# Attention steps moved in front of the state-weight products of a fused attention and two-FFN kernel

## The chip, the cores and the metric

One core of a Trainium2 chip runs the whole program. The metric is the device time of one execution in microseconds (us), lower is better, as the median of a few runs. Alongside, one execution was recorded by the hardware profiler; its rows give start and length of every instruction on each engine: PE (TensorE matmuls), DVE (VectorE), ACT (ScalarE), POOL (GpSimd), SP (SyncE, which issues DMAs here).

## What is computed

```python
def _attn_ref(x, state):             # x (8, 8, 512, 64), state (8, 8, 32, 64)
    scores = scale * x @ state^T;     a = softmax(scores);   xread = a @ state
    scores2 = scale * state @ x^T;    a2 = softmax(scores2); sread = a2 @ x
    return concatenate([xread, sread], axis=2)
x = attention output, transposed and reshaped to (4352, 512)
x = relu(x @ w_in)**2 @ w_out        # first FFN, 2048 wide
out = ((x @ w1) * (x @ w2)) @ w3 @ w_out2
```

## The kernel before, in words

The 4352 tokens are 8 batches of 512 rows (xread) and one block of 256 rows (sread of all batches), all held transposed. xread is never formed: since xread @ w_in = a @ (state @ w_in), `make_sw` multiplies the state of a batch by 512 columns of w_in (the **state weights**, SW), and `h_tile(c, f)` then multiplies the attention weights `aT` by them: six matmuls of 128x128 by 512 columns give tile f (of 16) of batch c before the relu. `act_h` makes relu (L534), square (L536) and the high part of a split (L537) of it on ACT, and the low part (L538, tile `ghl`, kept in the list `done`) on DVE. `y_tile` multiplies that by w_out, twelve matmuls.

**The loop.** The list `order` holds 96 pairs (c, f), and the loop (L834) makes one h tile per index i, then the y tile of an earlier index (two of them behind a state-weight group), so one index takes six plus twelve matmuls. The attention of a batch b is cut into steps (`att_steps`), which hang on the indices of this loop: `scores` (sixteen small matmuls on tiles of 64 rows by 32 columns of the array, into both banks of the PSUM tag "m", then two copies to the tiles S), `soft2`, `soft1a`, `soft1b` (softmax pieces on DVE and ACT), `a_T` (a turn on DVE and a split), `a2_T` (four PE transposes and a copy, once for each half r), `sread` (64 matmuls of 64 columns on tiles of 128 rows by 32 columns, a DVE copy to the tile sr) and `sread_T` (one PE transpose and a copy into x9T). `att_slots` gives for each batch a list of steps per index, counted from the index where the batch starts (32, 48, 60, 72, 85 for batches 3 to 7, 5 for batch 2); they are put into `late`, which runs at the end of an index. The steps stand alone: scores, each `a2_T`, sread and sread_T each come at an index of their own.

**State-weight groups.** At the indices 15, 23, 31, ... 87 (`pairs`) `sw_pair` makes two `make_sw` directly behind the h tile, and at index 95 two more are made for batches 6 and 7. Each of these groups is 32 small matmuls on tiles of 64 rows by 32 columns, and each `make_sw` fills two PSUM banks: the first takes both banks of tag "m", the second both banks of tag "h", in which `h_tile` also makes its product. So the second `make_sw` reuses the bank of the h tile just finished, which relu has to have read.

**What sets the order.** A planner puts each engine's instructions into one fixed order when the kernel is built: of what is ready in its own model of the time it takes what comes first in the program. `tc.issue_after(m)` adds that what follows on the engine of m stands behind m. On the chip every engine then takes its instructions in that order and waits at each for its semaphores. An x block for the scores is loaded by `load_xb` (eight DMAs on SP), turned on DVE by `turn_x`; the x block for sread is loaded by `load_xn` into the tag "X" (two buffers), one DMA on SP.

Of the kernel before, what the change touches and what calls it, by code (L numbers as in the profile page):

```python
# [20 lines left out]
def kernel(  # L21
# [17 lines left out]
    nc = tc.nc  # L39
    B, H, S, D = x.shape  # L40
# [5 lines left out]
    P = 128  # L46
# [3 lines left out]
    NF = DF // P  # L50
# [14 lines left out]
    BLK, ALONE = 2, 3  # L65
    PAIR = (B - 2, B - 1)
# [14 lines left out]
    def bank_m(name):  # L81
        return psum.tile([P, 512], F32, tag="m", bufs=2, name=name)

    def bank_h(name):
        return psum.tile([P, 512], F32, tag="h", bufs=2, name=name)
# [221 lines left out]
    def load_xn(b, g):  # L307
        t = att.tile([P, HG, J, D], F32, tag="X", bufs=2, name=f"X{b}_{g}")
        nc.sync.dma_start(t, x[b, g * HG:(g + 1) * HG].rearrange("h (j p) d -> p h j d", p=P))
        X[b, g] = t.rearrange("p h j d -> p j h d")  # L310
# [9 lines left out]
    def att_steps(b):  # L320
# [3 lines left out]
        v = {}  # L324
# [15 lines left out]
        def scores():  # L340
            pss = [bank_m("ps_s") for _ in range(G)]
            for k in range(HG):
                for r in range(G):
                    rows = slice(r * D, (r + 1) * D)
                    mm = nc.tensor.matmul(
                        pss[r][k * NS:(k + 1) * NS, :], stT[rows, b, k, :], xT[b, k][rows, :],
                        start=True, stop=True, tile_position=(r * D, k * NS),
                    )
            scored.append(mm)
            for r in range(G):  # L350
                pool, tag, bufs = (att, "S", 2) if b else (wpool, "wo", NF)
                s = pool.tile([P, 512], F32, tag=tag, bufs=bufs, name="S")
                last = nc.scalar.copy(s, pss[r])
                v["S", r] = s
            return last

        def soft2(r):
            nm = att.tile([P, 1], F32, tag="nm", bufs=2, name="nm")
# [65 lines left out]
                nc.tensor.transpose(ps[:, j * P:(j + 1) * P], e[:, j * P:(j + 1) * P], ident)  # L424
            nc.scalar.copy(e, ps)

        def sread():
            ps = bank_m("ps_r")
            for r in range(G):
                for j in range(J):  # L430
                    for k in range(HG):
                        nc.tensor.matmul(
                            ps[k * NS:(k + 1) * NS, r * D:(r + 1) * D],
                            v["a2", r][:, j * P + k * NS:j * P + (k + 1) * NS],
                            X[b, k // 2][:, j, 2 * (k % 2) + r, :],
                            start=(j == 0), stop=(j == J - 1), tile_position=(0, k * NS),
                        )
            t = att.tile([P, G * D], F32, tag="sr", bufs=1, name="sr")
            nc.vector.tensor_copy(t, ps[:, 0:G * D])
            v["sr"] = t  # L440

        def sread_T():
            ps = bank_m("ps_rT")
            nc.tensor.transpose(ps[:, 0:P], v["sr"], ident)
            (nc.vector.tensor_copy if b < ALONE else nc.scalar.copy)(
                x9T[:, :, b * NS:(b + 1) * NS], ps[:, 0:P].rearrange("p (k n) -> p k n", n=NS),
            )

        def step(f, *args):
            return lambda: f(*args)  # L450
# [3 lines left out]
            *([step(f, r) for r in range(G)] for f in (soft2, soft1a, soft1b, a_T, a2_T)),  # L454
            sread, sread_T,
        )

    def att_slots(b, parts=None):
        if b >= B:
            return [[] for _ in range(NF)]  # L460
        xp, sc, s2, s1a, s1b, at, a2t, sr, srt = att_steps(b)
        if parts is not None:
            parts.extend((xp, sc, s2, s1a, s1b, a2t, at))
        if b > ALONE + 1:
            return [
                [sc], [], [s2[0], s1a[0]], [s1b[0], s2[1]], [a2t[0]], [at[0], s1a[1]],
                [a2t[1]], [s1b[1]], [sr], [at[1]], [srt],
            ]
        if b > ALONE:
            return [  # L470
                [sc], [], [s2[0], s1a[0]], [],
                [s1b[0], s2[1]], [a2t[0]], [at[0], s1a[1]], [a2t[1]],
                [s1b[1]], [sr], [at[1]], [srt], [], [], [], [],
            ]
        if b == ALONE:
            return [
                [sc], [], [s2[0], s1a[0]], [], [s1b[0], s2[1]], [a2t[0]], [], [a2t[1]],
                [at[0], s1a[1]], [sr], [s1b[1]], [srt], [at[1]], [], [], [],
            ]
        return [  # L480
            [], [], [], [], [], [s1a[0]], [s1b[0]], [at[0], s1a[1]],
            [s1b[1]], [at[1]], [s2[0]], [a2t[0], s2[1]], [], [a2t[1]], [sr], [srt], [],
        ]

    SW = {}
    last_sw = []
# [228 lines left out]
    def sw(b, fg):  # L715
        return lambda: make_sw(b, fg)

    def sw_pair(b, fg):
        make_sw(b, fg)
        make_sw(b, fg + 1, banks=lambda r, name: bank_h(name))  # L720

    side = {i: [] for i in range(NF * B)}
    late = {}
# [28 lines left out]
    for g in range(G):  # L752
# [1 line left out]
        side[4 + g].append(lambda g=g: load_xb(2, g))  # L754
        side[8 + g].append(lambda g=g: turn_x(2, g))
        side[11 + g].append(lambda g=g: load_xn(2, g))
    att2 = []
    for i, steps in enumerate(att_slots(2, att2)):
        late[5 + i] = steps

    def scores_and_sw():
        with tc.issue_after(h_mms[-1].ins):
            att2[1]()
        with tc.issue_after(scored[-1].ins):
            sw_low.append(make_sw(1, 1, banks=lambda r, name: bank_h(name)))

    side[10].append(scores_and_sw)
    behind_y, sw_low = {10: [srt1]}, []
    for b, i0 in zip(range(ALONE, B), (32, 48, 60, 72, 85)):
        for i, steps in enumerate(att_slots(b)):  # L770
            late.setdefault(i0 + i, []).extend(steps)
        for g in range(G):
            side[i0 - 8 + g].append(lambda b=b, g=g: load_xb(b, g))
            side[i0 - (6 if b < B - 1 else 3) + g].append(lambda b=b, g=g: turn_x(b, g))
            side[i0 - 2 + g].append(lambda b=b, g=g: load_xn(b, g))
    for g in range(G):
        side[80 + 3 * g].append(lambda g=g: load_aT(PAIR[0], g))

# [54 lines left out]
    order += [(c, f) for c in range(3, PAIR[0]) for f in range(NF)]  # L833
    for i, (c, f) in enumerate(order):  # L834
        h_tile(c, f)
        if i in pairs:
            sw_pair(*pairs[i])
        if i + 1 == len(order):
            make_sw(c0, 0)
            make_sw(c1, 0, banks=lambda r, name: bank_h(name))  # L840

        gate = done[i - 3] if i >= 8 else first
        with tc.issue_after(gate.ins):
            for job in side.get(i, ()):
                job()
        pend.append((c, f))
        while len(pend) > (1 if i in pairs else 2):
            last_y = y_tile(*pend.pop(0))
            with tc.issue_after(last_y.ins):
                for job in behind_y.pop(i, ()):  # L850
                    job()
        with ExitStack() as order_of:
            if i >= 8:
                order_of.enter_context(tc.issue_after(done[i - 3].ins))
            if i == 10:
                order_of.enter_context(tc.issue_after(sw_low[0].ins))
            if 10 <= i < 16:
                order_of.enter_context(tc.issue_after(casts[-1].ins))
            if i == max(pairs):
                order_of.enter_context(tc.issue_after(relus[-1].ins))  # L860
            for job in late.get(i, ()):
                job()
# [901 lines left out]
```

## Time and profile before

| | |
|---|---|
| median of 3 runs | 1193.29 us (1192.48 to 1193.63) |
| the profiled execution | 1194.18 us, of which the span from first to last instruction is 1192.4 us |
| PE busy | 1181.7 us (99%), 6400 matmuls |
| DVE, ACT, POOL busy | 967.6 us (81%), 695.9 us (58%), 191.8 us (16%) |
| granted TensorE clock | 0.999 of full speed |
| chain that ended last | PE 94%, DMA 2%, DVE 2%, ACT 1% |

The times are to be read with one care: matmuls are pipelined, so a line of the timeline lasts longer than the step to the next line. What a stretch of PE costs is the difference between the start of its first line and the start of the line behind it.

### The profile page before, as it was taken

What the parts mean: (1) busy time and instruction counts of PE and PEld (TensorE: products, weight loads), DVE (VectorE), ACT (ScalarE), POOL (GpSimd) and SP (SyncE); (2) the same over time, 40 slices, a digit from 0 to 9 for tenths busy, and PEclk for the clock granted to TensorE, in tenths of its full rate; (3) what the DMA queues carried; (4) which work ended last, traced back from release to release, by engine and by line L of the source; (5) the groups of instructions that cost most, each with busy time, mean ns of one, the idle gap of its engine ahead of it and who ended that gap; (6) DMA issues with size and microseconds to landing.
All of it is one profiled execution on the core that took longest, in us unless ns stands there. A gap on an engine that the chain in (4) does not pass through costs nothing.

```text
span 1192.4 us, 17909 instructions
## 1 busy us (share of the span) xinstructions
PE 1181.7 (99%) x6400; PEld 950.4 (80%) x6400; DVE 967.6 (81%) x1729; ACT 695.9 (58%) x1263; POOL 191.8 (16%) x277
## 2 busy tenths in 40 slices
PE   8999999999999999999999999999999999999998
PEld 5677777777787777777788888888888888888888
DVE  7989877778888774676778986989898968988987
ACT  6777556565656565876867753636364635363642
POOL 0000013323331200012231000120101030313030
PEclk9999999999999999999999999999999999999999
DMA  8575768936885932447697676653514382666576
GB/s 253 140 231 190 184 212 238 198 120 175 173 203 169 245 130 102 114 109 114 98 184 243 235 195 159 106 146 67 142 56 121 131 230 67 165 98 158 90 124 178
DMA packets 204722, 187.58 MB, mean 157 GB/s; under 512 B 120648, under 2 KB 156232, under 8 KB 204104
## 3 DMA queue, kind: packets, MB, share of 16 engines
q1 hardware_dynamic: 155848, 111.70, 33.1%
q0 software_dynamic: 46768, 71.32, 28.7%
q10 hardware_dynamic: 2016, 3.41, 0.8%
q8 instruction: 50, 0.82, 0.3%
q14 instruction: 40, 0.33, 0.1%
HBM read 122.81 MB, written 82.44 MB: 172 GB/s over the span
## 4 chain that ended last, share of the span: by engine, by line
PE 94%; DMA 2%; DVE 2%; ACT 1%; issue 0%; POOL 0%; SPq 0%; DVEq 0%; POOLq 0%; ACTq 0%
PE y L594 22%; PE qa L1328 11%; PE qd L1328 7%; PE oa L1552 5%; PE ps_w L1132 4%; PE qc L1328 4%; PE qe L1328 4%; PE od L1552 3%; PE ps_sw L507 2%; PE qa L966 2%; PE ab L1407 2%; PE qd L966 2%; PE oc L1552 2%; PE oe L1552 2%; PE y L566 1%; PE po L1440 1%
## 5 line engine op out<-in xcount | busy, mean ns | idle before, releaser
L594 PE MATMUL y<-ghl,wo 128*128 128x512 f32 x1152 | 279.7, 392 | 0.1
L594 PEld LDWEIGHTS y<-ghl,wo 128*128 128x128 f32 x1152 | 214.5, 188 | 57.4 <-issue 12.6
L1328 PE MATMUL qa<-yq,wq 128*128 128x512 f32 x576 | 142.7, 389 | 0.0
L1337 ACT COPY s<-qa 128x512 f32<-128x512 f32 x96 | 56.4, 588 | 144.7 <-PE qa L1328 144.7
L538 DVE TENSOR_TENSOR ghl<-r,ghl 128x512 fp32r<-128x512 f32 (+1 forms) x112 | 72.5, 647 | 72.6 <-ACT ghl L537 63.8
L1328 PEld LDWEIGHTS qa<-yq,wq 128*128 128x128 f32 x576 | 108.0, 188 | 22.3
L1328 PE MATMUL qd<-yq,wq 128*128 128x512 f32 x384 | 97.4, 389 | 0.0
L1328 PEld LDWEIGHTS qd<-yq,wq 128*128 128x128 f32 x384 | 72.1, 188 | 15.0
L536 ACT ACTIVATE r<-r 128x512 f32<-128x512 f32 (+1 forms) x112 | 67.6, 603 | 4.2 <-DVE yo L605 1.4
L1237 DVE TENSOR_TENSOR yq<-yraw,yq 128x512 fp32r<-128x512 f32 x98 | 64.2, 683 | 6.1 <-ACT yq L1236 6.0
L537 ACT CAST ghl<-r 128x512 fp32r<-128x512 f32 (+1 forms) x112 | 66.2, 591 | 2.8
L1236 ACT CAST yq<-yraw 128x512 fp32r<-128x512 f32 x98 | 57.1, 622 | 5.5 <-DVE yraw L1242 3.5
L1502 POOL DMA_DIRECT2D osum<-turned x32 | 20.8, 655 | 183.1 <-DVE turned L1499 182.8
L1341 DVE TENSOR_TENSOR s<-qa,s 128x512 f32<-128x512 f32 x32 | 22.1, 689 | 33.2 <-ACT s L1337 33.1
L1328 PE MATMUL qc<-yq,wq 128*128 128x512 f32 x192 | 48.7, 389 | 0.0
L1328 PE MATMUL qe<-yq,wq 128*128 128x512 f32 x192 | 48.7, 389 | 0.0
L1132 PE MATMUL ps_w<-wo,w3T 128*128 128x512 f32 x192 | 44.1, 389 | 0.0
L1270 ACT CAST z<-q 128x512 fp32r<-128x512 f32 x64 | 37.4, 622 | 11.2 <-PE od L1563 5.3
L1275 DVE TENSOR_TENSOR q<-q,q 128x512 f32<-128x512 f32 x64 | 43.0, 683 | 0.1
L1328 PEld LDWEIGHTS qe<-yq,wq 128*128 128x128 f32 x192 | 36.0, 188 | 7.5
L1328 PEld LDWEIGHTS qc<-yq,wq 128*128 128x128 f32 x192 | 36.0, 188 | 7.5
L1132 PEld LDWEIGHTS ps_w<-wo,w3T 128*128 128x128 f32 x192 | 35.8, 188 | 7.5
(729 smaller groups left out, 2605.3 us busy)
## 6 DMA issues: line engine op xcount, KB each, us to landing
yraw<-yscr SPq DMA_DIRECT2D x56, 256.0 KB, 5.2
raw<-in_moe_w_out_dram SPq DMA_DIRECT2D x16, 512.0 KB, 4.6
yscr<-yo SPq DMA_DIRECT2D x32, 256.0 KB, 3.6
raw<-in_moe_w_dram POOLq DMA_DIRECT2D x64, 128.0 KB, 3.9
raw<-in_moe_w_dram POOLq DMA_DIRECT2D x16, 512.0 KB, 7.0
raw<-in_moe_w_in_dram SPq DMA_DIRECT2D x12, 512.0 KB, 4.5
xb<-in_x_dram SPq DMA_DIRECT2D x96, 64.0 KB, 3.1
X<-in_x_dram SPq DMA_DIRECT2D x12, 512.0 KB, 8.3
```

The source lines that it names most:

```text
L536: nc.scalar.activation(r[:, :n], r[:, :n], ACTF.Square)
L537: casts.append(nc.scalar.copy(t[:, HI, :n], r[:, :n]))
L538: done.append(nc.vector.tensor_tensor(out=t[:, LO, :n], in0=r[:, :n], in1=f32(t[:, HI, :n]), op=ALU.subtract))
L594: mm = nc.tensor.matmul(y_ps[c, d][:, :n], wo_t[f][:, wi, d * P:(d + 1) * P], t[:, gi, :n], start=(f == f0 and k == 0), stop=(f == f1 - 1 ...
L966: nc.tensor.matmul(ps[d], wt[:, wi, d * P:(d + 1) * P], v[:, kt, gi, :], start=(first and kt == 0 and k == 0), stop=(last and kt == 1 and ...
L1132: mm = nc.tensor.matmul(ps, t[:, wi, (j % 4) * P:(j % 4 + 1) * P], wo2_t[j][:, vi, :], start=(j == 0 and k == 0), stop=(j == N1 - 1 and k ...
L1236: left["yq"] = nc.scalar.copy(t[:, HI], src(kt))
L1237: nc.vector.tensor_tensor(out=t[:, LO], in0=src(kt), in1=f32(t[:, HI]), op=ALU.subtract)
L1275: return nc.vector.tensor_tensor(out=t, in0=a, in1=b, op=ALU.subtract)
L1328: mm = nc.tensor.matmul(ps, W[w, kt][:, wi, m * P:(m + 1) * P], Y[v, kt][:, vi, :], start=(first and kt == 0 and k == 0), stop=(last and k ...
L1337: left["copy"] = nc.scalar.copy(t, ps)
L1552: mms.append(nc.tensor.matmul(ps[d], lhs[:, wi, d], Z[v, idx][:, vi, :], start=(first and idx == 0 and k == 0), stop=(last and idx == NB - ...
```

## The change

Scores, sread and sread_T are taken out of `late` and are called by the new `sw_group`, directly behind the h tile and in front of the two `make_sw` of a group, each of them chained behind the one before it on PE. The first `make_sw` of a group now takes the banks of tag "h" and the second those of tag "m". The second copy to S goes to DVE for batches 3 to 7. Both `a2_T` of a batch come at one index. sread_T and one sread take a bank of tag "h" where scores follow in the same group. The indices of the other steps, and of the loads and turns of x, move by some places.

```diff
@@ scores
-                last = nc.scalar.copy(s, pss[r])
+                last = nc.vector.tensor_copy(s, pss[r]) if r and b >= ALONE else nc.scalar.copy(s, pss[r])
                 v["S", r] = s
-            return last
+            return mm if b >= ALONE else last
@@ sread, sread_T: a parameter bank=bank_m, and both return their last matmul
@@
-    def sw_pair(b, fg):
-        make_sw(b, fg)
-        make_sw(b, fg + 1, banks=lambda r, name: bank_h(name))
+    def sw_group(steps, sws):
+        mm = h_mms[-1]
+        for step in steps:
+            with tc.issue_after(mm.ins):
+                mm = step()
+        for n, (b, fg) in enumerate(sws):
+            with tc.issue_after(mm.ins):
+                make_sw(b, fg, banks=None if n else lambda r, name: bank_h(name))
+                mm = last_sw[-1]
@@ batch 2
+    late.update({
+        10: [s1a2[0]], 11: [s1b2[0]], 12: [at2[0], s1a2[1]], 13: [s1b2[1]], 14: [at2[1]],
+        15: [s22[0]], 16: [s22[1]], 18: a2t2,
+    })
+    with_sw = {i: [] for i in (*pairs, NF * PAIR[0] - 1)}
+    with_sw[23].append(sr2)
+    with_sw[31].append(lambda: srt2(bank_h))
@@ batches 3 to 7
+    plan = {
+        3: (31, (33, 35, 37, 40, 42, 44)), 4: (47, (49, 51, 52, 53, 54, 57)), 5: (63, (65, 66, 67, 68, 69, 70)),
+        6: (71, (73, 74, 75, 76, 78, 80)), 7: (87, (89, 90, 91, 92, 93, 94)),
+    }
+    for b, (i0, (i1, i2, i3, i4, i5, i6)) in plan.items():
+        xpb, scb, s2, s1a, s1b, at, a2t, sr, srt = att_steps(b)
+        with_sw[i0].append(scb)
+        for i, steps in (
+            (i1, [s2[0], s1a[0]]), (i2, [s1b[0], s2[1]]), (i3, a2t), (i4, [at[0], s1a[1]]), (i5, [s1b[1]]), (i6, [at[1]]),
+        ):
+            late.setdefault(i, []).extend(steps)
+        if i0 + 8 in [v[0] for v in plan.values()]:
+            with_sw[i0 + 8].append(lambda sr=sr: sr(bank_h))
+        else:
+            with_sw[i0 + 8].append(sr)
+        if i0 + 16 in with_sw:
+            with_sw[i0 + 16].insert(0, lambda srt=srt: srt(bank_h))
+        else:
+            late.setdefault(i0 + 8, []).append(srt)
...
-            side[i0 - 2 + g].append(lambda b=b, g=g: load_xn(b, g))
+            side[i0 + 1 + g].append(lambda b=b, g=g: load_xn(b, g))
@@ the loop
         h_tile(c, f)
-        if i in pairs:
-            sw_pair(*pairs[i])
-        if i + 1 == len(order):
-            make_sw(c0, 0)
-            make_sw(c1, 0, banks=lambda r, name: bank_h(name))
+        if i in with_sw:
+            b, fg = pairs.get(i, (None, None))
+            sw_group(with_sw[i], ((b, fg), (b, fg + 1)) if i in pairs else ((c0, 0), (c1, 0)))
```

Worked out, the groups hold: 15 nothing, 23 sread of batch 2, 31 sread_T 2 and scores 3, 39 sread 3, 47 sread_T 3 and scores 4, 55 sread 4, 63 sread_T 4 and scores 5, 71 sread 5 and scores 6, 79 sread_T 5 and sread 6, 87 sread_T 6 and scores 7, 95 sread 7 (sread_T 7 stays in `late` at 95).

## Rows read from the trace of the kernel before

**Rows 1.** Busy time of each engine from 100 to 490 us, the stretch of the change
```profile
core 0: us, PE busy (x) PEld busy (x) DVE busy (x) ACT busy (x) POOL busy (x), PEclk, DMA share, GB/s
100.00:490.00 390.00, 390.00 (x2399) 302.89 (x2398) 293.60 (x576) 234.11 (x416) 84.96 (x142) 1.00 0.68 180
```

**Rows 2.** PE timeline, indices 30 to 34: a state-weight group (31), scores alone (behind 32)
```profile
start us, us, engine line op out<-in xcount [idle before <-releaser]
167.35 1.52 PE L549 MATMUL ph__1939<-aT,sw 128*128 128x512 f32 x6
168.71 2.88 PE L594 MATMUL y<-ghl,wo 128*128 128x512 f32 x12
171.43 1.52 PE L549 MATMUL ph__1978<-aT,sw 128*128 128x512 f32 x6
172.88 1.95 PE L507 MATMUL ps_sw<-win,stT 64*32 64x512 f32 x32
174.75 5.73 PE L594 MATMUL y<-ghl,wo 128*128 128x512 f32 x24
180.33 1.52 PE L549 MATMUL ph__2049<-aT,sw 128*128 128x512 f32 x6
181.78 1.09 PE L345 MATMUL ps_s<-xT,stT 64*32 64x512 f32 x16
182.80 1.65 PE L549 MATMUL ph__2089<-aT,sw 128*128 128x512 f32 x6
...
187.03 1.52 PE L549 MATMUL ph__2136<-aT,sw 128*128 128x512 f32 x6
```

**Rows 3.** PE timeline, scores of batch 2 directly in front of one make_sw
```profile
77.94 1.09 PE L345 MATMUL ps_s<-xT,stT 64*32 64x512 f32 x16
78.83 1.06 PE L507 MATMUL ps_sw<-win,stT 64*32 64x512 f32 x16
```

**Rows 4.** PE timeline, an sread alone
```profile
220.02 2.88 PE L594 MATMUL y<-ghl,wo 128*128 128x512 f32 x12
222.83 1.10 PE L432 MATMUL ps_r<-X,e 128*32 128x64 f32 x64
223.86 1.65 PE L549 MATMUL ph__2541<-aT,sw 128*128 128x512 f32 x6
225.35 2.88 PE L594 MATMUL y<-ghl,wo 128*128 128x512 f32 x12
```

**Rows 5.** PE timeline, half an sread in front of a make_sw
```profile
56.51 0.65 PE L432 MATMUL ps_r<-X,e 128*32 128x64 f32 x32
57.10 1.56 PE L507 MATMUL ps_sw<-win,stT 64*32 64x512 f32 x12
```

**Rows 6.** PE timeline, an sread_T alone, and the second h tile behind it
```profile
232.16 0.27 PE L444 MATMUL ps_rT<-ident,sr 128*128 128x128 f32 x1
...
236.40 1.52 PE L549 MATMUL ph__2665<-aT,sw 128*128 128x512 f32 x6
```

**Rows 7.** PE timeline, one a2_T alone, and the two h tiles behind it
```profile
203.35 0.60 PE L424 MATMUL ps_a<-ident,e 128*128 128x128 f32 x4
203.71 1.64 PE L549 MATMUL ph__2305<-aT,sw 128*128 128x512 f32 x6
...
207.91 1.52 PE L549 MATMUL ph__2331<-aT,sw 128*128 128x512 f32 x6
```

**Rows 8.** ACT timeline beside the scores of rows 2
```profile
181.88 0.60 ACT L534 ACTIVATE r<-ph__2049 128x512 f32<-128x512 f32 x1 [4.52 <-PE ph__2049 L549]
...
183.18 0.62 ACT L537 CAST ghl<-r 128x512 fp32r<-128x512 f32 x1
183.70 1.07 ACT L353 COPY S<-ps_s 128x512 f32<-128x512 f32 x2
```

**Rows 9.** DVE timeline beside the same scores
```profile
183.83 0.69 DVE L538 TENSOR_TENSOR ghl<-r,ghl 128x512 fp32r<-128x512 f32 x1 [0.51 <-ACT ghl L537]
```

**Rows 10.** A DVE copy of a whole PSUM bank (the y results): count, ns min/median/max
```profile
L605 DVE COPY yo<-y x10: 647/682/691, 149.9 to 482.7; 128x512 f32<-128x512 f32 x10
```

**Rows 11.** DVE timeline, the copy behind the sread of rows 4
```profile
224.57 0.28 DVE L439 COPY sr<-ps_r 128x128 f32<-128x128 f32 x1
```

**Rows 12.** DMA issues of load_xn: count, KB each, us to landing
```profile
X<-in_x_dram SPq DMA_DIRECT2D x12, 512.0 KB, 8.3
```

More of the change, by code (lines that the diff above doesn't have):

```diff
@@ L425, in a2_T, with sread @@
             nc.scalar.copy(e, ps)
-        def sread():
-            ps = bank_m("ps_r")
+        def sread(bank=bank_m):
+            ps = bank("ps_r")
             for r in range(G):
@@ L431, in sread @@
                     for k in range(HG):
-                        nc.tensor.matmul(
+                        mm = nc.tensor.matmul(
                             ps[k * NS:(k + 1) * NS, r * D:(r + 1) * D],
@@ L440, in sread, with sread_T @@
             v["sr"] = t
-        def sread_T():
-            ps = bank_m("ps_rT")
-            nc.tensor.transpose(ps[:, 0:P], v["sr"], ident)
+            return mm
+        def sread_T(bank=bank_m):
+            ps = bank("ps_rT")
+            mm = nc.tensor.transpose(ps[:, 0:P], v["sr"], ident)
             (nc.vector.tensor_copy if b < ALONE else nc.scalar.copy)(
@@ L447, in sread_T @@
             )
+            return mm
         def step(f, *args):
@@ L456, in att_steps @@
         )
[L458 to L483, printed above, removed]
     SW = {}
@@ L756 @@
         side[11 + g].append(lambda g=g: load_xn(2, g))
-    att2 = []
-    for i, steps in enumerate(att_slots(2, att2)):
-        late[5 + i] = steps
+    xp2, sc2, s22, s1a2, s1b2, at2, a2t2, sr2, srt2 = att_steps(2)
+    late.update({
[5 more added lines that the diff above has]
+    with_sw[31].append(lambda: srt2(bank_h))
     def scores_and_sw():
         with tc.issue_after(h_mms[-1].ins):
-            att2[1]()
+            sc2()
         with tc.issue_after(scored[-1].ins):
@@ L768 @@
     behind_y, sw_low = {10: [srt1]}, []
-    for b, i0 in zip(range(ALONE, B), (32, 48, 60, 72, 85)):
-        for i, steps in enumerate(att_slots(b)):
-            late.setdefault(i0 + i, []).extend(steps)
+    plan = {
[17 more added lines that the diff above has]
+            late.setdefault(i0 + 8, []).append(srt)
         for g in range(G):
```

## The prediction

> **What bounds the kernel now.** I read the busy shares first, then the stretch of the change by windows, then the PE timeline around each step that moves, and last ACT and DVE beside them. From 100 to 490 us PE is busy for all 390 of 390 us, with DVE at 294 and ACT at 234 [rows 1]: PE waits for nothing here, so only work or gaps on PE itself can be taken out, and any wait that is put in counts in full. After 490 us the change leaves everything as it is, so what is gained or lost before that moves the end by the same amount.
>
> The timeline shows where PE loses time without waiting. An h tile takes 1.36 us (167.35 to 168.71) and a y tile 2.72 (168.71 to 171.43) [rows 2]. Around every visit to small array tiles more goes by than the visit's own matmuls need: the h tile before a visit takes 1.45 (171.43 to 172.88), and after scores an h and a y tile take 4.23 (182.80 to 187.03) where 4.08 is usual [rows 2].
>
> **The change part by part: what it saves.** Scores alone: from 180.33 to 187.03 are 6.70 us, of which two h tiles and a y tile explain 5.44; the visit costs 1.26 [rows 2]. A group of two make_sw takes 1.87 (172.88 to 174.75), a visit of half as many matmuls, the scores, 1.02 (181.78 to 182.80) [rows 2]: sixteen more small matmuls in an open visit cost 0.85. That scores in front of make_sw behave so is seen once, for batch 2: make_sw begins 0.89 after the scores [rows 3]. Saved: 0.41 for each of batches 3 to 7, **2.05 us**.
>
> An sread alone: the y tile before it takes 2.81 (0.09 too much), the visit 1.03, the h tile behind it 1.49 (0.13 too much), so 1.25 [rows 4]. In front of a group the entry is shared and the exit falls away, if the step from its tiles (128 rows) to those of make_sw (64 rows) is free. Half an sread in front of a make_sw takes 0.59 (56.51 to 57.10) for 32 matmuls [rows 5], more than half of 1.03 because each visit has one end, but no extra before make_sw beyond that. Saved 0.22 for each of batches 2 to 7, **1.32 us**. The rule against this stands in the Trainium skill, TensorEngine Tiling (Array Packing), section Key Properties: changing the tiling mode, not just the tile, drains the engine. By it the six reads would still pay one change of mode inside the group, 0.09 each, and the forecast would be 0.5 us higher; rows 5 speak against a large such price.
>
> sread_T alone: 232.16 to 236.40 are 4.24 where 4.08 is usual, 0.16 [rows 6]. In front of scores or sread no row shows it; between nothing and all of 0.16 is saved. I take half, since its exit goes but its own matmul stays: five (batches 2 to 6), **0.40 us**; the ends are 0 and 0.8.
>
> Two a2_T at one index: one alone costs 0.48 (203.35 to 207.91 is 4.56 against 4.08), of which 0.36 is its own time until the h tile starts [rows 7]. The second one then saves between 0 and 0.12; I take the middle, 0.06, six times, **0.36 us** (0 to 0.72).
>
> Sum of savings: 4.13 us.
>
> **What it costs.** The new groups put a read of PSUM between matmuls on PE. In a group with scores the second make_sw takes the banks of tag "m", out of which the two S copies must come first. It is due 0.89 + 0.85 = 1.74 after the scores begin. On ACT, where scores follow an h tile directly, the order was relu, square, cast of that tile and then the S copies, which began at 183.70 though the scores had ended at 182.87 [rows 2, 8]; the new scores follow an h tile too, and program order puts the tile's three ahead. The first copy takes about 0.6 (an estimate, from the cast of the same size, 0.62 [rows 8]) and ends at 184.30, 2.52 after the scores' start at 181.78: PE waits 0.78. That holds for the groups at 31, 47, 63 and 87, where nothing long stands in front of the scores: **3.1 us**. The lower bound is a copy that begins as the scores end: 182.87 + 0.6 is 1.69 after their start, no wait. The upper bound is the second copy, now on DVE, standing behind the low part `ghl` of the same tile: that begins at 183.83 and takes 0.69 [rows 9], and a copy of a bank takes 0.68 on DVE [rows 10], so 185.20, a wait of 1.68 each, 6.7 in all. I take 0.78, because DVE had a gap of 0.51 before `ghl` [rows 9] into which the copy fits. The Trainium skill says it as a rule, in the same page, section PSUM Bottleneck: tiling makes TensorE faster but not the emptying of PSUM, which may become the bottleneck, and both ScalarE and VectorE should do it. The trace agrees: 0.85 us of matmuls against copies of 0.6 and more behind other work.
>
> At 71 an sread stands in front of the scores, so the second make_sw is due 1.03 later; the ACT copy is then in time and the DVE copy, behind `ghl`, 0.65 late at worst: I take **0.3**.
>
> At 15 nothing stands in front, and the first make_sw now takes tag "h", whose second bank relu must read first. Relu begins 0.10 after a visit starts and takes 0.60 [rows 2, 8]: PE waits **0.7**. Before, the second make_sw took these banks, 0.85 later. In all other groups at least 0.85 of scores or 1.03 of sread lies between, so this wait is covered by them.
>
> At 23, 39, 55, 79 and 95 the second make_sw needs the bank of the sread. It is due 1.03 + 0.85 = 1.88 after the sread's start; the DVE copy ended 2.02 after it (224.57 + 0.28 against 222.83) [rows 4, 11]. I take 0.14 each, **0.7 us**; the ends are 0 and 1.14 (behind `ghl`, by rows 9 as above).
>
> Five copies of 0.68 come to DVE (3.4 us) and leave ACT: free, both have room [rows 1]. Moved loads: `load_xn` (one DMA per half) is issued two to six indices later and lands in 8.3 us [rows 12], while six indices or more of 4.08 us lie between it and its sread; it waits for the X buffers of the sread before, which ends an index or more earlier, so SP is not held up. `load_xb` (eight DMAs per half) and `turn_x` move by one to three indices either way and stay two or more ahead of the scores. The softmax steps move too, but keep an index between `soft2` and `a2_T`. If any of these came late, PE would wait in the group; I price them at nothing.
>
> Costs: 3.1 + 0.3 + 0.7 + 0.7 = 4.8. **The sum**: 4.8 less 4.13, 0.67 us more than the profiled execution's 1194.18, that is 1194.85. The median of the runs is 0.89 below that execution, so I predict 1194.0.
>
> **The rivals.**
> A, the copies come at once: the planner puts S copies and sread copies ahead of square and cast, so that only the 0.7 at index 15 is left: 4.13 - 0.7 = 3.4 saved, 1189.9 us. For it: an idle DVE and the gap between relu and square. Against it: rows 8.
> B, slower: the DVE copies stand behind `ghl` of the h tile. Then 6.7 + 0.65 + 0.7 + 0.7 = 8.75 is paid against 4.13, 1197.9 us. It decides as soon as two of the four groups are so. For it: the program has `ghl` before the copy. Against it: `ghl` waits for the cast, and the scores end before the cast does.
> C, the planner sees the waits and puts y matmuls between the two make_sw. Each split costs a visit of its own (1.26 against 0.85, so 0.41) at 15, 31, 47, 63 and 87 in place of the waits there: 2.05 + 0.3 + 0.7 = 3.05 against 4.13, 1192.2 us. For it: at 57 us one make_sw was split like that, 12 matmuls of 16 standing together [rows 5].
> D, the steps don't stand where the program puts them, and little changes: 1193.3.
>
> **How the numbers follow.** A change of 0.2% (2.4 us) is about what a measurement of this kernel can tell from none. The forecast has 0.42 (0.33 within the bound, 0.03 faster, 0.06 slower, as its unknown terms fall), A 0.25 (0.23 faster, 0.02 within), B 0.18 (0.16 slower, 0.02 within), C 0.12 (0.11 within, 0.01 faster), D 0.03 within. So faster 0.27, same 0.51, slower 0.22. The range 1190.0 to 1197.5 leaves out about half of A and half of B, 0.2 in all; the forecast's own range is 1192 to 1196.
>
> **What would show it.** Right: on PE scores, sread and sread_T stand directly in front of the 32 matmuls of a group, with no entry or exit of their own; in the groups at 31, 47, 63 and 87 a gap of about 0.8 between the two make_sw, put down to the ACT copy of S; at 15 a gap of 0.7 inside the first make_sw behind relu; a2_T rows of eight. Wrong: gaps of 1.7 with DVE's S copy as releaser (B), no gap at all (A), or y matmuls inside a group (C).

## The result and the profile after

The changed kernel takes 1203.18 us (median of 6 runs, 1201.25 to 1207.29) against 1193.46 beside it: a ratio of 1.0086, with a 95% interval of 1.0068 to 1.0103. It is slower, by 9.7 us, and outside the range that was given. The profiled execution took 1203.43 us, 9.25 more than that of before.

PE, which waited for nothing in the stretch of the change [rows 1], now does. The same view of the changed kernel, 100 to 490 us:

```profile
100.00:490.00 390.00, 385.07 (x2357) 296.98 (x2356) 291.14 (x576) 224.48 (x399) 82.66 (x140) 1.00 0.67 175
```

PE is busy for 385.07 of 390 us, and DVE and ACT are no busier than before: nothing became a bound by its work. The granted clock is 1.00 in both, the upper level of 2.4 GHz. "Busy" tells only a part here: PE is idle for 4.93 us in this row, while 13.18 us are lost by the steps from start to start (below), so a part of its standing is counted as busy. The waits view of PE names who is waited for (engine, tile and line, releaser: us in total, times, longest):

```profile
PE ps_sw L482 <- DVE S L353: 2.7, 2, 2.0
PE ps_sw L482 <- ACT S L353: 1.6, 3, 0.5
...
PE ps_sw L482 <- DVE x9T L446: 0.6, 1, 0.6
```

None of the three is there before. They are copies out of PSUM: scores, sread and sread_T hold banks that the group's `make_sw` needs next.

**The group at 47** shows the pattern that 63 and 87 repeat. PE timeline of the changed kernel (a start to the next start is what a step costs):

```profile
249.85 1.53 PE L524 MATMUL ph__2726<-aT,sw 128*128 128x512 f32 x6
251.21 0.27 PE L445 MATMUL ps_rT<-ident,sr 128*128 128x128 f32 x1
251.41 1.09 PE L345 MATMUL ps_s<-xT,stT 64*32 64x512 f32 x16
252.29 1.06 PE L482 MATMUL ps_sw<-win,stT 64*32 64x512 f32 x16
253.88 1.93 PE L482 MATMUL ps_sw<-win,stT 64*32 64x512 f32 x16 [0.52 <-ACT S L353]
255.74 5.51 PE L569 MATMUL y<-ghl,wo 128*128 128x512 f32 x23
```

Its ACT timeline beside it, which answers to rows 8, and its DVE timeline, which answers to rows 9:

```profile
251.41 0.60 ACT L509 ACTIVATE r<-ph__2726 128x512 f32<-128x512 f32 x1 [2.17 <-PE ph__2726 L524]
251.90 0.26 ACT L446 COPY x9T<-ps_rT 128x128 f32<-128x128 f32 x1
252.05 0.64 ACT L511 ACTIVATE r<-r 128x512 f32<-128x512 f32 x1
252.72 0.62 ACT L512 CAST ghl<-r 128x512 fp32r<-128x512 f32 x1
253.25 0.58 ACT L353 COPY S<-ps_s 128x512 f32<-128x512 f32 x1
```
```profile
253.38 0.69 DVE L513 TENSOR_TENSOR ghl<-r,ghl 128x512 fp32r<-128x512 f32 x1 [2.79 <-ACT ghl L512]
253.98 0.69 DVE L353 COPY S<-ps_s 128x512 f32<-128x512 f32 x1
```

The last scores matmul ends at 252.50 (251.41 + 1.09). DVE idles for 2.79 us until 253.38, in which its copy of S (0.69) would just have fitted after the scores; but the copy stands behind `ghl` of the h tile, which waits for the cast on ACT. So the first bank, which ACT empties, comes free at 253.83 and the second at 254.67. The 32 matmuls take 3.45 (252.29 to 255.74) where 1.88 is their length (478.68 to 480.56 at index 95, where nothing waits, below): 1.57 lost.

**The group at 31** loses most, 3.89 us (5.77 from 174.84 to 180.61). PE, then DVE:

```profile
174.84 1.02 PE L482 MATMUL ps_sw<-win,stT 64*32 64x512 f32 x2
176.48 1.09 PE L482 MATMUL ps_sw<-win,stT 64*32 64x512 f32 x16 [0.62 <-DVE x9T L446]
179.60 1.09 PE L482 MATMUL ps_sw<-win,stT 64*32 64x512 f32 x14 [2.02 <-DVE S L353]
180.61 5.74 PE L569 MATMUL y<-ghl,wo 128*128 128x512 f32 x24
```
```profile
175.20 0.69 DVE L167 CUSTOM_DVE_ANT_0 cw<-raw,cw 128x1024 uint16<-128x1024 uint16 x1
175.80 0.42 DVE L150 TENSOR_SCALAR raw<-raw 128x512 int32<-128x512 uint32 x1
176.14 0.29 DVE L446 COPY x9T<-ps_rT 128x128 f32<-128x128 f32 x1
176.72 0.43 DVE L162 TENSOR_SCALAR cw<-raw 128x512 f32<-128x512 f32 x1 [0.29 <-DMA wscr<-cw]
...
178.26 0.68 DVE L513 TENSOR_TENSOR ghl<-r,ghl 128x512 fp32r<-128x512 f32 x1
178.86 0.68 DVE L353 COPY S<-ps_s 128x512 f32<-128x512 f32 x1
```

Here weight conversions (L150 to L167, the side jobs) stand ahead of x9T, and one that first waits for a store of an earlier conversion (`wscr<-cw`) stands ahead of S (0.29 us; an earlier one of 1.56 at 168.45 is taken up at E8). At 71 three conversion pieces stand between `ghl` (366.20) and S (367.95). At 39 it is the copy of sread that is late, behind two conversion pieces and `ghl`; PE, then DVE:

```profile
214.41 1.10 PE L432 MATMUL ps_r<-X,e 128*32 128x64 f32 x64
215.44 3.06 PE L482 MATMUL ps_sw<-win,stT 64*32 64x512 f32 x32
218.43 5.74 PE L569 MATMUL y<-ghl,wo 128*128 128x512 f32 x24
```
```profile
216.47 0.69 DVE L513 TENSOR_TENSOR ghl<-r,ghl 128x512 fp32r<-128x512 f32 x1
217.07 0.28 DVE L439 COPY sr<-ps_r 128x128 f32<-128x128 f32 x1
```

PE gives 3.06 for the 32 matmuls in one row and names no waiter there: a hole of single matmuls has to be found by the steps from start to start (2.99 in place of 1.88), not by the row's bracket.

**What was gained** is there too. PE at 95, a group with its sread in front and no wait, and a visit of eight for two `a2_T`:

```profile
207.96 1.04 PE L424 MATMUL ps_a<-ident,e 128*128 128x128 f32 x8
208.75 1.64 PE L524 MATMUL ph__2311<-aT,sw 128*128 128x512 f32 x6
...
477.65 1.10 PE L432 MATMUL ps_r<-X,e 128*32 128x64 f32 x64
478.68 1.95 PE L482 MATMUL ps_sw<-win,stT 64*32 64x512 f32 x32
480.56 3.02 PE L569 MATMUL y<-ghl,wo 128*128 128x512 f32 x12
```

The account, term by term, in us. Measured savings come from steps such as these, measured costs from the length of each group's 32 matmuls less 1.88; both sums together agree with the shift of PE between index 15 and the end of the loop (9.77 - 0.25 = 9.52).

| term | predicted | measured |
|---|---|---|
| scores in front (0.88 for 1.26), 5 times | -2.05 | -1.90 |
| sread in front (1.03 for 1.25), 6 times | -1.32 | -1.32 |
| sread_T in front (0.11 for 0.16), 5 times | -0.40 | -0.25 |
| a2_T in pairs (0.93 for 0.96), 6 times | -0.36 | -0.18 |
| S copies late at 31, 47, 63, 87 | +3.1 | +8.60 (3.89, then 1.57 each) |
| S copy late at 71 | +0.3 | +1.77 |
| relu late at 15 | +0.7 | +0.75 |
| sread copies late | +0.7 | +2.06 (23: 0.39, 39: 1.11, 55: 0.56; 79, 95: none) |
| net | +0.67 | +9.53 |

### The profile page after: what moved, and what is told of

The parts are those of the page before. It is cut to its first block, busy times and chain, and to the rows that moved or that the text cites. A ratio compares the mean times of both kernels' runs of the same rounds, so it can differ in the third digit from the quotient of the medians.

```text
span 1201.6 us, 17929 instructions
## 1 busy us (share of the span) xinstructions
PE 1187.1 (99%) x6400; PEld 953.8 (79%) x6400; DVE 969.9 (81%) x1734; ACT 694.1 (58%) x1258; POOL 191.8 (16%) x277
## 3 DMA queue, kind: packets, MB, share of 16 engines
q0 software_dynamic: 46768, 71.32, 28.5%
## 4 chain that ended last, share of the span: by engine, by line
PE 90%; DMA 3%; DVE 3%; ACT 2%; issue 2%; POOL 1%; SPq 0%; DVEq 0%; POOLq 0%; ACTq 0%
PE y L569 19%; PE qa L1328 11%; PE qd L1328 7%; PE oa L1552 5%; PE ps_w L1132 4%; PE qc L1328 4%; PE qe L1328 4%; PE od L1552 3%; PE ps_sw L482 2%; PE qa L966 2%; PE ab L1407 2%; PE qd L966 2%; PE oc L1552 2%; PE oe L1552 2%; PE y L541 1%
## 5 line engine op out<-in xcount | busy, mean ns | idle before, releaser
L482 PE MATMUL ps_sw<-win,stT 64*32 64x512 f32 (+1 forms) x528 | 44.2, 584 | 6.5 <-DVE S L353 2.7
L239 POOL DMA_DIRECT2D raw<-in_moe_w_dram x64 | 35.1, 587 | 55.6 <-DVE cw L167 34.3
L92 DVE TENSOR_TENSOR sw<-ps_sw,sw 128x512 fp32r<-128x512 f32 (+1 forms) x66 | 40.8, 664 | 1.4 <-ACT sw L91 1.2
```

What stands on the lines that cost most here:

```text
L482: mm = nc.tensor.matmul(pss[r][k * NS:(k + 1) * NS, cols], st_of(b)[rows, k, :], win_t[fg][rows, k, cols], start=True, stop=True, tile_pos ...
```

## The experiments

The theory (O): the loss lies in the order of work on DVE and ACT, which puts the PSUM copies behind `ghl` and conversions. The rivals: the mixing of small tiles with full matmuls costs it (M), what is put back to make room comes late for its own readers (conversions: C, `ghl`: G), a moved transfer (D). These letters are the experiments' own and not those of the rivals in the prediction. As a yardstick I use the distance from the start of the h tile at an index to the start of the next h tile, from the PE timelines (8.90 is a group with nothing in front and no wait; before the change a lone `a2_T` stands in the distance at 39 and a lone sread_T in that at 71; the last line is the sum of the three tiles behind the group at 31, 9.52 when nothing waits and 1.26 more with scores among them; E2, E4 and E7 are told in the text; in E3 one y tile of 31, 2.72, stands in the last line in place of the line of 31):

| index | before | after | E1 | E3 | E5 | E6 | E8 | E9 | E10 |
|---|---|---|---|---|---|---|---|---|---|
| 15 | 8.90 | 9.66 | 9.66 | 9.66 | 8.90 | 9.66 | 9.66 | 8.90 | 8.90 |
| 23 | 8.90 | 10.32 | 10.31 | 9.93 | 9.93 | 10.33 | 9.66 | 8.90 | 8.90 |
| 31 | 8.90 | 13.79 | 11.48 | 9.52 | 13.68 | 17.35 | 12.03 | 13.01 | 9.11 |
| 39 | 9.26 | 11.05 | 11.09 | 9.93 | 9.93 | 11.07 | 11.05 | 9.93 | 9.93 |
| 47 | 8.90 | 11.47 | 11.11 | 10.15 | 10.13 | 10.15 | 11.49 | 10.15 | 10.13 |
| 71 | 9.05 | 12.58 | 11.40 | 11.26 | 11.39 | 12.63 | 12.60 | 11.40 | 11.39 |
| 87 | 8.90 | 11.49 | 11.15 | 16.67 | 10.14 | 10.14 | 11.51 | 10.17 | 10.15 |
| 32 to 34 | 10.78 | 9.52 | 9.52 | 14.31 | 12.45 | 9.52 | 10.07 | 11.33 | 10.78 |

**E1, both S copies on ACT**

```diff
-                last = nc.vector.tensor_copy(s, pss[r]) if r and b >= ALONE else nc.scalar.copy(s, pss[r])
+                last = nc.scalar.copy(s, pss[r])
```

> Edit: both S copies of a scores visit go to ScalarE again, as before the change; all else as in the changed kernel. Theory O (the loss is the order of work on the two copy engines: the VectorE copy of S stands behind the subtraction of the group's own h tile, though VectorE is idle ahead of it): the waits of 2.02 us at the group at index 31 and of 0.65 at 71 shrink to about the 0.5 us that ScalarE's second copy ends behind its first, those at 47, 63 and 87 (0.71 us for the second half) likewise to about 0.4; together about -4.5 us, so some 1198.7 us against the changed kernel's 1203.2. Theory M (the loss lies in putting small tiles and full-array matmuls in one visit, or in the moved loads of X, and the order of the copies is only a bystander): no change, 1203.2 us within 1.

Measured: 1198.88 us, ratio to before 1.0043 (1.0029 to 1.0057). The five groups fall as O had it, 31 by 2.31, 71 by 1.18, 47, 63 and 87 by some 0.36 each. So the choice of DVE for the second copy costs 4.3 us by itself, and M, which expected no change, falls for this part; the 5 us by which E1 stays above the kernel before are not yet decided by it. The second copy is better off behind the first on ACT than on an engine that is free but has other work ahead of it in its order.

**E2, the side jobs behind the copies** (`copies` collects the PSUM copies of the steps)

```diff
-        with tc.issue_after(gate.ins):
+        with ExitStack() as order_of:
+            order_of.enter_context(tc.issue_after(gate.ins))
+            for copy in copies[n0:] if i in with_sw else ():
+                order_of.enter_context(tc.issue_after(copy.ins))
             for job in side.get(i, ()):
                 job()
```

> Edit: the side jobs of an index that has a group (the hi/lo conversions of weights and x, and the like) may issue only behind the PSUM copies of the group's steps; square, cast and subtraction of the h tile stay where they are. Theory O: the part of the waits that stood behind conversions goes: 0.39 us at index 23, about 2.5 at 31, 0.3 to 0.6 at 55, 1.1 at 71, and the 1.57 us at each of 47, 63 and 87, which stand behind the subtraction alone, stay. Together about -4.4 us, some 1198.8 us. Theory M: no change, 1203.2 us within 1. A third, C (the conversions that are now late make the next weight groups late): 1203 or above, with new waits of h or y matmuls on the conversions.

Measured: 1211.0 us, 1.0138 (1.0123 to 1.0154). C holds: the 32 matmuls at 31 lose 2.38 us in place of 3.89, but the tiles behind wait. (The distance at 31 is 9.57 here, yet one of its two y tiles, 2.72, now comes behind the start of the next h tile; with the three tiles behind, 31 takes 23.56 us, against 23.31 in the changed kernel.) The waits view of PE:

```profile
PE ps_s L347 <- DVE xT L304: 2.6, 1, 2.6
...
PE y L572 <- ACT ghl L515: 1.5, 1, 1.5
PE y L572 <- ACT wo L91: 1.4, 1, 1.4
```

y matmuls wait for weights whose conversion was pushed back, and scores of batch 7 for the turn of its x. The conversions can't all make way.

**E3 and E4, copies first; and at 15 the m ring first**

```diff
+        def rest():
...
+        if hold:
+            held.append(rest)
+        else:
+            rest()
```

`rest` makes square, cast and `ghl` of the h tile; where it is held, `sw_group` runs it, issued behind the steps' copies. E3 has the side jobs behind the copies too, as E2. E4 adds the first `make_sw` on tag "m" where no step stands in front.

> Edit: in every group that has a step in front, relu stays where it is, and square, cast and subtraction of the group's own h tile, and the index's side jobs, may issue only behind the PSUM copies of the group's steps. Theory O: the excess of the groups' state-weight matmuls over their nominal length, 13.2 us in the changed kernel, falls to 1.5 to 2.5 us (0.75 at 15, which has no step, 0.1 to 0.3 at each other), the savings of about 3.7 us stay, and the time is 1191.5 to 1192.5 us, below the kernel before at 1193.5. Theory M: the excess stays for the most part, 1202 us or above. Theory G (g is late then: the y matmuls two steps on wait for the subtraction): the excess goes, but the y matmuls behind the groups wait, and the time is 1194 to 1198 us.

> Edit: as in the run with the copies first, and the group at index 15, which has no step in front, takes the bank of the m ring first and the h bank second, as before the change. Theory O: the 0.75 us that the matmuls at 15 wait for relu to free the h bank goes, so 0.75 us less than the run with the copies first: 1190.8 to 1191.8 us. If the h bank is late for the second half as well, no difference.

Measured: 1205.54 us (1.0101, 1.0087 to 1.0116) and 1205.62 (1.0101, 1.0083 to 1.0119). Both miss O's time by 13 to 14 us, though most groups do what O says: 10.15 at 47, 9.93 at 23 and 39; at 31 the 32 matmuls of E3 still lose 1.42. What they gain is lost behind them, as in E2 (31 to 34 is no shorter than after, and scores at 87 wait 2.9 us for xT; of the 16.67 us there a part is also the clock, granted at 0.50, the lower level of 1.2 GHz, from 444.9 to 448.3, after that wait). G is right about the kind of loss, not about its source: one y wait of 1.7 us is for `ghl`, most of the others (2.5 us) for converted weights. In E4 the group at 15 is back at 8.90; the medians, in which late conversions vary more than that, don't show it.

**E6, the copies ahead of square, cast and `ghl` at 47, 63 and 87 alone**

```diff
-        h_tile(c, f)
+        h_tile(c, f, hold=i in (47, 63, 87))
```

> Edit: in the groups at 47, 63 and 87 alone, square, cast and subtraction of the group's own h tile may issue only behind the S copies; all else as in the changed kernel. Theory O: these three groups fall from 11.47 to 11.49 us to the 10.15 seen with the copies first, 4.0 us together, so some 1199.2 us. Theory M (the small tiles' visit itself is that long): no change, 1203.2 us.

Measured: 1199.36 us, 1.0062 (1.0049 to 1.0075), the forecast to 0.2 us. The profiled execution, at 1203.07 the slowest of the five, has the 4.0 us of the three groups too, but lost 3.55 at 31. PE at 47:

```profile
254.58 1.09 PE L347 MATMUL ps_s<-xT,stT 64*32 64x512 f32 x16
255.47 2.17 PE L485 MATMUL ps_sw<-win,stT 64*32 64x512 f32 x32
257.57 4.62 PE L580 MATMUL y<-ghl,wo 128*128 128x512 f32 x19
```

The 32 matmuls take 2.10 where they took 3.45, with the same matmuls and the same banks: the order of the copies is the cause, and M is left with 0.22 at most. The edit moves both copies, ACT's from behind square and cast and DVE's from behind `ghl`, so it doesn't tell one from the other.

At 31, where every engine's order is that of the changed kernel, this execution took 17.35 us in place of 13.79. PE stood 1.14 us for x9T and 3.10 for S, not 0.62 and 2.02, since DVE waited longer for the stores (2.08 and 1.37 us, not 1.56 and 0.29). That makes 1.60 of the 3.55. The rest is the clock, which fell to its lower level of 1.2 GHz while PE stood; the fourteen matmuls behind took 1.89 in place of 1.01 and the two y tiles 6.66 in place of 5.58. The PE row of the longer wait, and the windows view of 178 to 185 us (the third column from the right is the granted clock, the last two are DMA):

```profile
180.78 1.96 PE L485 MATMUL ps_sw<-win,stT 64*32 64x512 f32 x14 [3.10 <-DVE S L355]
```
```profile
178.00:185.00 7.00, 4.22 (x20) 2.07 (x21) 6.93 (x15) 2.61 (x6) 2.54 (x4) 0.51 0.95 321
```

**E7, scores alone again**

```diff
-        with_sw[i0].append(scb)
+        late.setdefault(i0 + 1, []).append(scb)
```

> Edit: the scores of batches 3 to 7 leave the groups and stand alone again behind the next h tile (indices 32, 48, 64, 72, 88); sread, sread_T and the pairs of a2_T stay where the change puts them. Theory O: without the two banks of the scores the groups at 47, 63 and 87 fall from 11.5 to about 9.1 us (8.9 of the kernel before and 0.2 for sread_T), 71 from 12.6 to about 10.2, 31 from 13.8 to about 9.8 (x9T still late by 0.6); five lone visits of 1.26 us come back. Together about -7.2 us, 1196 us. If instead the sread part carries the loss, the time stays above 1200 us.

Measured: 1198.44 us, 1.0048 (1.0035 to 1.0061). 47, 63 and 87 fall to 9.15, as expected; 31 stays at 10.69 and 71 at 12.02 (an x9T and an sread copy late), so only two thirds of the 7.2 us come. The scores part of the change, at first sight its largest saving, costs 4.7 us on the whole.

**E5, prompt copies with the side jobs where they were**

As E4, without E2's edit, and with some copies on ACT (sr at 23, 39, 55 and 71, S at 31 and 71, x9T of batch 2):

```diff
-                last = nc.vector.tensor_copy(s, pss[r]) if r and b >= ALONE else nc.scalar.copy(s, pss[r])
+                last = nc.vector.tensor_copy(s, pss[r]) if r and b in (4, 5, 7) else nc.scalar.copy(s, pss[r])
...
-            nc.vector.tensor_copy(t, ps[:, 0:G * D])
+            copies.append((nc.vector.tensor_copy if b > 5 or b < 2 else nc.scalar.copy)(t, ps[:, 0:G * D]))
```

> Edit: square, cast and subtraction of a group's own h tile may issue only behind the PSUM copies of the group's steps, as in the run with the copies first, but the side jobs keep their old place. Copies that would stand behind conversions on VectorE go to ScalarE, behind relu: sr at 23, 39, 55 and 71, both S copies at 31 and 71, x9T of batch 2 at 31. At 15 the m ring comes first. Theory O (order on the copy engines, nothing else): by the tile-to-tile distances of the runs so far, a group with sread is down to 9.93 us, with sread_T and scores to 10.15, at 31 to 9.6 to 9.9, at 71 to 11.2 to 11.6, at 15 to 8.90, and no wait appears elsewhere; against the changed kernel that is some 12 us less, 1191 us within 0.8, below the kernel before at 1193.5 to 1194. Theory G (a later subtraction starves the y matmuls): the groups are short but y waits behind them, as in the run with the copies first at index 73; 1194 to 1198 us.

Measured: 1195.46 us, 1.0018 (1.0009 to 1.0027). All groups are as O had them but 31 and the tiles behind it, which are some 7 us too long together. PE and DVE there:

```profile
183.78 2.92 PE L535 MATMUL ph__2059<-aT,sw 128*128 128x512 f32 x6 [2.76 <-DVE sw L92]
```
```profile
178.24 0.43 DVE L162 TENSOR_SCALAR cw<-raw 128x512 f32<-128x512 f32 x1 [3.17 <-DMA wscr<-cw]
```

DVE stands 3.17 us in front of a conversion that needs an earlier store landed, and the splits of the group's own state weights (L92) stand behind it. Of the 7 us, 2.9 lie in the tiles behind, where nothing waits: there the clock was at its lower level after PE had stood for 2.76 us (1.00 from 170 to 182 us, then this), so the first h tile took 2.72 in place of 1.36. The windows view:

```profile
182.90:189.90 7.00, 6.12 (x15) 4.80 (x16) 3.97 (x10) 4.31 (x8) 1.37 (x3) 0.51 0.63 152
```

In the kernel before, DVE waits for such a store too, but with the four splits ahead of it, so that nobody on PE notices:

```profile
176.15 2.48 DVE L92 TENSOR_TENSOR sw<-ps_sw,sw 128x512 fp32r<-128x512 f32 x4
...
180.03 0.43 DVE L162 TENSOR_SCALAR cw<-raw 128x512 f32<-128x512 f32 x1 [1.06 <-DMA wscr<-cw]
```

**E8, early X; E9, prompt copies and early X**

```diff
-    with_sw[23].append(sr2)
+    late[19] = [sr2]
...
-            side[i0 + 1 + g].append(lambda b=b, g=g: load_xn(b, g))
+            side[(i0 + 1 if b > ALONE else i0 - 2) + g].append(lambda b=b, g=g: load_xn(b, g))
```

> Edit: sread of batch 2 goes back to its own place at index 19, and the two X loads of batch 3, which take the buffers that it frees, are issued ahead of the loads of xb as before the change; all else, the order of the copies too, as in the changed kernel. Theory D (at 31 the loss is a moved transfer: the X loads now run at 150 to 168 us in place of before 130, beside the stores of converted weights; VectorE waits for those stores, and x9T and S stand behind the conversions): the group at 31 falls from 13.8 us to about the 11.5 of 47 and 63, the other groups stay, 1200.5 us. Theory O without it (order of copies only): 31 stays at 13 us or more, and only the 0.4 us of the group at 23 goes, 1202.8 us.

> Edit: the prompt copies of the earlier run and this early X together; sread_T of batch 2 too stands alone again, at index 20. Theory O with D: no wait of over 0.4 us is left in any group; 31 at about 9.8 us (8.9 and 0.88 of scores), and no wait behind it. From index 34 on the run with prompt copies gained 1.6 us on the kernel before; with 0.4 at 31 this makes 2.0 us less than the kernel before, some 1191 us. Theory O alone: 31 and the h and y tiles behind it stay some 5 us too long, 1195 us as in the run with prompt copies.

Measured: E8 1201.4 us, 1.0072 (1.0057 to 1.0086). That interval, 1199.6 to 1203.0 us, holds the times of both theories; the trace has to decide. There 31 falls by 1.76 of the 2.3 that D expected. Stores of converted weights issued between 150 and 170 us (count, KB, median us to landing), of before, after and E8:

```profile
wscr<-cw POOLq DMA_DIRECT2D x2, 256.0 KB, 4.6
```
```profile
wscr<-cw POOLq DMA_DIRECT2D x3, 256.0 KB, 5.6
```
```profile
wscr<-cw POOLq DMA_DIRECT2D x2, 256.0 KB, 3.7
```

The changed kernel issues the X loads of batch 3 at 156.2 and 156.7 us, where the kernel before does at 124.2 and 126.4 and E8 at 123.9 and 127.1. Their buffers are free from about 138.8 on, when sread of batch 2 at 23 ends; until 156 they stand in SP's order behind loads of xb and of weights and stores of y. The DMA engines are then busy for 0.82 of 150 to 170 us, against 0.63 before and 0.57 in E8. The store issued at 162.8 lands in 5.6 us, the one in its place in E8 (164.5) in 2.3. In the changed kernel DVE stands for its store, ahead of the conversions, x9T and S of 31:

```profile
168.45 0.43 DVE L162 TENSOR_SCALAR cw<-raw 128x512 f32<-128x512 f32 x1 [1.56 <-DMA wscr<-cw]
```

This repeats: in all five executions with the X loads at 155 to 157 us (after, E1, E5, E6, E7) that store took 5.4 to 6.7 us and DVE stood for 1.35 to 2.71, and in the three with the loads at 123 to 127 (E8, E9, E10) it took 2.3 and DVE did not stand there. So D is shown as a part of the loss at 31, not as all of it; its size, 1.76, is that of one execution, and E6 shows that stores alone can move the group by 1.6. E8 moves sread of batch 2 and the place of the loads in SP's order together, so it doesn't tell which of the two made the loads late.

E9: 1194.22 us, 1.0013 (1.0000 to 1.0026), 3 us above its forecast. 31 and what follows stay long, for the same reason as in E5, with a DMA wait that is longer still:

```profile
180.05 0.43 DVE L162 TENSOR_SCALAR cw<-raw 128x512 f32<-128x512 f32 x1 [5.46 <-DMA wscr<-cw]
```

DVE gets past it at 180 us, as it did before the change. It matters because holding `ghl` back let the conversion pass it, and the splits with it.

**E10, nothing in front at 31**

```diff
-        with_sw[i0].append(scb)
+        if b > ALONE:
+            with_sw[i0].append(scb)
+        else:
+            late.setdefault(i0 + 1, []).append(scb)
```

> Edit: as in the run with prompt copies and early X, and the group at 31 has no step in front: the scores of batch 3 stand alone again behind the h tile of index 32, as before the change. Theory Q (what is left at 31 is VectorE standing in a store of converted weights, ahead of the splits of the group's own state weights, because the subtraction that was put back let a conversion pass it): without the step the splits stand ahead of that conversion, as in the kernel before; the group takes 8.90 us again in place of 13.0, the tiles behind it lose their 1.8 us of waits, the lone scores cost 1.26 in place of 0.88. That is 5 us less than the run before it: 1189.3 us, 3.5 us below the kernel before. If the stores themselves are late for the group whatever the order, 31 to 34 stay 3 us or more too long, 1192.5 us or above.

Measured: 1191.08 us against 1193.47 beside it, 0.9981 (0.9972 to 0.9990): faster than both kernels. 31 takes 9.11 and the tiles behind it 10.78, as Q had it; the time is 1.8 us above its forecast, whose 5 us had been read from the profiled execution of E9, 1.2 us slower than E9's median. By its own terms they were 4.6: 4.1 and 1.8 less 1.26, since the 0.88 is in the 4.1 already.

By the account above E10 should gain 1.43 us (savings of 3.00 less 1.57 still lost in its groups), and from the h tile at 15 to the end of the group at 95 its trace is 1.46 shorter than before. The medians differ by 2.4. The two profiled executions differ by a further 1.15 ahead of index 15, where the granted clock was 0.50 from 28.5 to 31.9 us before and 1.00 in E10; the changed kernel and E1, whose orders are the same up to there, differ as much (99.80 and 98.55 us at the start of index 15). So 1.4 us of the gain are accounted for; that the edit brings the rest isn't shown.

From 100 to 490 us its waits view of PE is empty, and DVE at 47 has the copy ahead of its `ghl`:

```profile
245.94 0.69 DVE L355 COPY S<-ps_s 128x512 f32<-128x512 f32 x1 [2.05 <-PE ps_s L347]
...
247.76 0.65 DVE L519 TENSOR_TENSOR ghl<-r,ghl 128x512 fp32r<-128x512 f32 x1
```

## Why the prediction was wrong

**The bound was right.** PE had no slack from 100 to 490 us, every wait that was put in counted in full, and what was lost by index 95 is the difference at the end (9.8 of PE's start there, 9.25 in the profiled times).

**The savings were right**, 4.13 predicted and 3.65 measured, the difference mostly in the two small terms that no row showed. The doubted price did not come on top: from sread's tiles to those of `make_sw` PE takes 1.03, the same as sread alone in front of an h tile [rows 4] and as sread in front of scores (364.15 to 365.18). The Trainium skill, TensorEngine Tiling (Array Packing), section Key Properties, says that a change of the tiling mode drains the engine. All three of these steps change the mode, so the rows show that the one to `make_sw` is no dearer than the others, not that it is free.

The rivals A, C and D of the prediction did not come: the steps stand where the program puts them, the copies are late, and in no group is there a y matmul among the 32.

**The step that failed** is the term "I take 0.78, because DVE had a gap of 0.51 before `ghl` [rows 9] into which the copy fits". ACT's side of it was right: at 47 its copy of S ended 2.42 us after the scores began (253.83 less 251.41), 2.52 by the forecast, and the first matmul for that bank came 0.74 late (253.88 against 252.29 + 0.85). DVE's side was wrong. The gap was there, and larger (2.79), but the copy came behind `ghl` in DVE's fixed order, so DVE stood at `ghl` through the gap and the copy came after it; that raised the loss from 0.74 to 1.57. The prediction used program order for ACT ("program order puts the tile's three ahead") and let it go for DVE, where the same order puts `ghl` ahead. Rival B said what happened at 47, 63 and 87, 1.68 each, measured 1.57; it had a chance of 0.18. E1 changes DVE's copy alone and E6 both copies; no run puts only DVE's copy into the gap, so the split of the 1.57 is read from the rows.

**Two more terms were too small for one reason.** Of the 8.86 us by which the net was missed, 5.50 lie in the term for 31, 47, 63 and 87 (3.11 of them at 31), 1.47 at 71, 1.36 at the sreads, 0.48 in the savings and 0.05 at 15. B itself came out at 8.75 us of costs where 13.18 were paid, since conversions too stand between the steps' matmuls and their copies: at 31, at 71 (0.3 predicted, "at worst 0.65", measured 1.77) and at the sreads, where 0.14 was taken from a copy that stood alone in the kernel before [rows 11] and had nothing ahead of it. The upper end given there, 1.14 behind `ghl`, is what 39 paid (1.11).

**A cost put at nothing was not nothing.** The moved X loads came in time for their sread, as reckoned; what the text didn't ask is what else they delay. The later X loads of batch 3 met the stores of converted weights, for which DVE waits, ahead of the copies (E8: 1.56 us of standing less, 1.76 less at 31).

**The term at 15** was right (0.75), and could be had back by the order of the banks (8.90 in E5, E9 and E10).

Emptying the two banks of scores with both engines cost 4.3 us more here than with ACT alone (E1), for the copy's place in DVE's order; with the copies ahead of square, cast and `ghl` the same two engines leave 0.22 us of wait (E6, 2.10 against 1.88). The Trainium skill, TensorEngine Tiling (Array Packing), section PSUM Bottleneck, advises to use both. The runs agree where the order lets them work, and not where it doesn't; of the order the section says nothing.

**Still open**: how much of the 3.89 us at 31 the moved loads bring, as stores that land later moved the group by nearly as much between two executions of one order (1.60 against 1.76); what the clock's falls, seen in four profiled executions between 100 and 490 us (E2, E3, E5, E6), do to the medians; and whether scores and sread_T in front of the group at 31 could be had with only the conversion behind the splits put back, which was not tried.

## What to carry to other kernels

When a step is moved in front of work that reuses its PSUM banks, the price is set by the place of its copy in the order of the copying engine, not by that engine's idle time: list what the program puts ahead of the copy, with what each of these waits for, a DMA above all. Put the copy ahead of what nobody waits for soon (here square, cast and `ghl`), and leave ahead of it what is needed at once; pushing everything back cost more than it brought (E2 1211.0 us, E3 1205.5, the changed kernel 1203.2). A moved load has to be priced by the transfers that it now runs beside as well as by its own reader.

## What the runs showed that was not expected

The step from sread's tiles of 128 rows to tiles of 64 rows took no longer than the step to a full-array h tile (1.03 us for the visit in both). The group at 31 took 13.79 and 17.35 us in two executions in which every engine had the same order up to there. Stores that landed later made 1.60 us of the difference; the lower clock, which came while PE stood, made the rest. So waits on a DMA in the middle of an engine's order made this kernel not only slower but less steady.
